# Two attention blocks on one core: the first 256 tokens transposed on TensorE, weight and x loads rescheduled

## The chip, the core and the metric

The kernel runs on one core of a Trainium2 chip. The metric is the time of one execution on the device, in microseconds (us). The core's engines run side by side and wait for each other through semaphores: TensorE (PE) multiplies and transposes, its weight loads shown apart as PEld; VectorE (DVE) and ScalarE (ACT) work on SBUF and PSUM; GpSimd (POOL) only makes an identity matrix here; the sync engine's queue (SPq) issues every DMA, plain copies and DMA transposes alike, in one order.

## The reference

Two independent attention blocks, A and B, of equal shapes; their outputs stand side by side in the last dimension.

```python
# per block: x [8, 144, 640], k_cache and v_cache [8, 32, 512, 128], wq [640, 4096], wo [4096, 640], bf16
q = (x @ wq).reshape(B, Sq, H, Dh).transpose(0, 2, 1, 3)
scores = einsum("bhqd,bhkd->bhqk", q, k_cache) * (Dh ** -0.5)
p = softmax(scores, axis=-1)
o = einsum("bhqk,bhkd->bhqd", p, v_cache)
return o.transpose(0, 2, 1, 3).reshape(B, Sq, H * Dh) @ wo
```

Each K and each V head is used once, for 144 queries, so the caches (2 x 2 x 33.5 MB) are streamed from HBM.

## The kernel before

The work is cut into 64 groups: block, then batch, then four groups of eight heads. So groups 0 to 31 are block A and 32 to 63 block B, and four groups make one batch. A group does the following (`attention_group`, L380):

- four projections of two heads each, ten matmuls into `ps_q` (L396), scaled into `qt_sb` by ScalarE (L407). They read a quarter of wq (`wq_sb`, one quarter for each g) and the transposed x (`xT_sb`, five chunks of 128 features by 1152 tokens);
- scores of 128 queries for each head (L483), and of the last 16 queries of all eight heads together (L425, eight small matmuls, once in a group);
- the row maximum on VectorE (L355), the exponential on ScalarE (L359), reciprocal and scaling on VectorE (L371, L376);
- transposes of the probabilities on TensorE into `ps_pt` (L504, L450), copied out by VectorE (L520, L465);
- the product with V into `ps_o` (L531), copied out by ScalarE (L544, L545).

The output projection of a batch (`outproj_ops`: L578 for the first 512 columns, L593 for the last 128, copies at L605 and L611, stores at L619 and L625) is cut into small items, which a queue hands out as filler between the attention steps, one at every second call of `fill`. The last 16 queries of all eight batches are projected together as one more "remainder" at the end of each block.

Loads go through four helpers: `load_wq` (L288, issue at L294), `load_wo` (L298, L304), `load_xT` (L308, L315: five DMA transposes of 576 tokens, half of a block's) and `load_kv` (L321: for each of the two halves of a group one DMA transpose of four K heads, L335, and one plain load of four V heads, L340). K has a ring of four slots, that is two groups; V has six.

No order is written out by hand. Every operation is handed to a small planner (`_Sched`) with what it reads and writes, an estimated duration, and a priority that is mostly its number in the program. The planner fixes, before the launch, the order of each engine's instructions and of the DMA queue, looking over the next 24 of each. On the chip each engine works through its list and waits on semaphores; an issue whose buffer is not free holds back everything behind it on the DMA queue.

Where the weight and x loads stand in the program decides their place in the queue:

- start: `load_xT(0, 0)`, then wq quarter 0 of A, then K and V of group 0; wq quarter g ahead of group g (L655 to L658);
- the second half of A's xT ahead of group 12 (L660); wo quarter hg of A ahead of group 4 + hg (L662);
- wq quarter g of B right behind group 28 + g (L705);
- the first half of B's xT behind group 15 (L707), the second half behind group 31 (L709), that is just ahead of group 32;
- the four wo quarters of B as queue items behind the whole remainder of A (L710 to L712).

Of the kernel before, what the change touches and what calls it, by code (L numbers as in the profile page):

```python
# [22 lines left out]
NPT_BANKS = 2  # L23
SCHED_WINDOW = 24
MODEL_ONLY = False
PRIO = {"OPa": 150, "OPb": 150, "Qp": -40, "Qe": -40}
OPA_HEADS = 4
FILL_STRIDE = 2
OPB_HEADS = 8
_DBG = {}  # L30

# [24 lines left out]
class _Sched:  # L56
# [36 lines left out]
    def schedule(self, engines, window=24):  # L93
# [22 lines left out]
        while remaining:  # L116
            best = None
            for e in engines:
                lst = per_eng[e]
                n = len(lst)  # L120
                cnt = 0
                i = pos[e]
                cand = None
                tf = t_eng[e]
                while i < n and cnt < window:
                    oi = lst[i]
                    if not done[oi]:
                        cnt += 1
                        rt = ready_time(ops[oi])
                        if rt < INF:  # L130
                            if rt + LEAD <= tf:
                                cand = (tf, oi, 0.0)
                                break
                            st = rt if rt > tf else tf
                            if cand is None or st < cand[0] - 1e-9:
                                cand = (st, oi, PENALTY.get(e, 0.0))
                    i += 1
                if cand is not None and (best is None or cand[0] < best[0] - 1e-9):
                    best = (cand[0], cand[1], e, cand[2])
# [37 lines left out]
def bass_concat_heads__gqa_block_cached__mha_block_cached__near_ridge_kernel(  # L177
# [34 lines left out]
    XH = 2 if NB % 2 == 0 else 1  # L212
    BPH = NB // XH

    NK = 4
    NV = 6
    NP = 8
    NT = 12
    NQG = 2
    NOB = 2  # L220
    NOS = 2

    S = _Sched()

    with ExitStack() as st:
# [36 lines left out]
        for e in ("pe", "act", "dve", "pool"):  # L262
            sem(("eng", e))

        def setup_ops():
            def f_ones(g):
                return g.memset(ones_sb[:], 1.0)
# [17 lines left out]
                                        for g in range(NG) for pi in range(4)],  # L285
                  dur=_dve_ns(2 * H * 128, 4), name="zero_otr")

        def load_wq(blk, hg):  # L288
            wq = blks[blk][3]
            src = wq.rearrange("(c p) n -> p c n", p=128)[:, :, hg * 1024:(hg + 1) * 1024]  # L290
            dst = wq_sb[:, :, hg * 1024:(hg + 1) * 1024]

            def f(e):
                return e.dma_start(dst, src)  # L294
            S.add("sp", f, writes=[("wq", hg)], dur=200, dma=(("wq", hg), 128 * NCH * 1024 * 2, "pl"),
                  name="wq%d.%d" % (blk, hg))

        def load_wo(blk, hg):  # L298
            wo = blks[blk][4]
# [5 lines left out]
            S.add("sp", f, writes=[("wo", hg)], dur=200, dma=(("wo", hg), 128 * 8 * D * 2, "pl"),  # L305
                  name="wo%d.%d" % (blk, hg))

        def load_xT(blk, half):  # L308
            x = blks[blk][0]
            xf = x.rearrange("b q d -> (b q) d")  # L310
            t0 = half * BPH * SQ
            t1 = (half + 1) * BPH * SQ
            for c in range(NCH):
                def f(e, c=c):
                    return e.dma_start_transpose(xT_sb[:, c, t0:t1], xf[t0:t1, c * 128:(c + 1) * 128])  # L315
                S.add("sp", f, writes=[("xT", half, c)], dur=200,
                      dma=(("xT", half, c), (t1 - t0) * 256, "tr"), name="xT%d.%d.%d" % (blk, half, c))

        kv_ctr = [0]

        def load_kv(blk, b, g):  # L321
            kc = blks[blk][1]
            vc = blks[blk][2]
            slots = []
            for s2 in range(2):
                h0 = 8 * g + 4 * s2
                kslot = kv_ctr[0] % NK
                vslot = kv_ctr[0] % NV
                kv_ctr[0] += 1
                slots.append((kslot, vslot))  # L330
                ksrc = kc[b, h0:h0 + 4].rearrange("h k d -> (h k) d")
                vsrc = vc[b, h0:h0 + 4].rearrange("h (p c) d -> p h (c d)", p=128)

                def fk(e, kslot=kslot, ksrc=ksrc):
                    return e.dma_start_transpose(kt_sb[:, kslot, :], ksrc)  # L335
                S.add("sp", fk, writes=[("KT", kslot)], dur=200, dma=(("KT", kslot), 4 * SK * 256, "tr"),
                      name="K%d.%d.%d.%d" % (blk, b, g, s2))

                def fv(e, vslot=vslot, vsrc=vsrc):
                    return e.dma_start(v_sb[:, vslot, :, :], vsrc)  # L340
                S.add("sp", fv, writes=[("V", vslot)], dur=200, dma=(("V", vslot), 4 * SK * 256, "pl"),
                      name="V%d.%d.%d.%d" % (blk, b, g, s2))
            return slots

        tile_ctr = [0]
        sbank_ctr = [0]
        ptbank_ctr = [0]

        def softmax_me(sbank, tag):
            ts = tile_ctr[0] % NT  # L350
            pslot = (tile_ctr[0] // 1) % NP
            tile_ctr[0] += 1

            def f_m(v):
                return v.tensor_reduce(nm_sb[:, ts:ts + 1], ps_s[:, sbank, :], AXL.X, ALU.max, negate=True)  # L355
            S.add("dve", f_m, reads=[("PSS", sbank)], writes=[("nm", ts)], dur=_dve_ns(512), name="M" + tag)

            def f_e(a):
                return a.activation(p_sb[:, pslot, :], ps_s[:, sbank, :], ACTF.Exp,  # L359
                                    bias=nm_sb[:, ts:ts + 1], scale=1.0, accum_out=rs_sb[:, ts:ts + 1])  # L360
            S.add("act", f_e, reads=[("PSS", sbank), ("nm", ts)], writes=[("P", pslot), ("rs", ts)],
                  dur=_act_ns(512, 1, True), name="E" + tag)
            return ts, pslot

        def softmax_rn(tiles, tag):
# [7 lines left out]
                  writes=[("rr", t0 + i) for i in range(n)], dur=68 + 2 * n, name="R" + tag)  # L373
            for i, (ts, pslot) in enumerate(tiles):
                def f_n(v, ts=ts, pslot=pslot):
                    return v.tensor_scalar(p_sb[:, pslot, :], p_sb[:, pslot, :], rr_sb[:, ts:ts + 1], None, ALU.mult)  # L376
                S.add("dve", f_n, reads=[("rr", ts), ("P", pslot)], writes=[("P", pslot)],
                      dur=_dve_ns(512, 4, 1), name="N%s.%d" % (tag, i))

        def attention_group(blk, b, g, gi, fill, heads_done):  # L380
            gs = gi % NQG
            bs = b % NOB
            slots = load_kv(blk, b, g)
            half = b // BPH
            tg = "%d.%d.%d" % (blk, b, g)

            for pi in range(4):
# [3 lines left out]
                def f_qp(t, pi=pi):  # L391
                    ins = None
                    for uu in range(2):
# [6 lines left out]
                                start=(c == 0), stop=(c == NCH - 1),  # L400
                            )
                    return ins
                S.add("pe", f_qp, reads=[("wq", g)] + [("xT", half, c) for c in range(NCH)],
                      writes=[("PSQ",)], dur=2 * NCH * _mm_ns(SQ), name="Qp%s.%d" % (tg, pi))

                def f_qe(a, pi=pi, off=off):
# [147 lines left out]
        def outproj_ops(blk, b, acc=None, acc_res=("PSOUT",)):  # L554
# [33 lines left out]
            def mk_b(k):  # L588
                def go():
                    def f(t):  # L590
                        ins = None
                        for h in range(OPB_HEADS * k, OPB_HEADS * (k + 1)):
                            ins = t.matmul(acc[:, 0:D2], lhs(h), wo_sb[:, h, 512:D],  # L593
                                           start=(h == 0), stop=(h == H - 1))
                        return ins
# [56 lines left out]
            load_wo(blk, hg)  # L652
            wo_loaded.add((blk, hg))

        before(0, lambda: load_xT(0, 0))  # L655
        before(0, lambda: load_wq(0, 0))
        for g in range(1, NG):
            before(g, lambda g=g: load_wq(0, g))  # L658
        if XH == 2:
            before(BPH * NG - NG, lambda: load_xT(0, 1))  # L660
        for hg in range(NHG):
            before(NG + hg if NB > 1 else NG - 1, lambda hg=hg: do_load_wo(0, hg))  # L662

        queues = [[], []]

# [21 lines left out]
        for blk in range(2):  # L687
            for b in range(NB):
# [6 lines left out]
                for g in range(NG):  # L695
# [3 lines left out]
                        queues[1].extend(outproj_ops(blk, NB, acc=ps_q, acc_res=("PSQ",)))  # L699
                    fill_state[0] = 0  # L700
                    fill_state[1] = FILL_STRIDE
                    attention_group(blk, b, g, gi, fill, heads_done)
                    gi += 1
                    if blk == 0 and b == NB - 1:
                        load_wq(1, g)  # L705
                if blk == 0 and XH == 2 and b == BPH - 1:
                    load_xT(1, 0)  # L707
                if blk == 0 and b == NB - 1:
                    load_xT(1, XH - 1)  # L709
                    queues[0].extend(outproj_ops(blk, NB))  # L710
                    for hg in range(NHG):
                        queues[0].append((1, -1, 0, None, lambda hg=hg: do_load_wo(1, hg), NB - 1))  # L712
        heads_done[(1, -1)] = 0
        while queues[0] or queues[1]:
            if not pop_filler():
# [27 lines left out]
        for o in ops:  # L743
            if o.dma is not None and o.dma[0][0] in ("out", "outr"):
                out_final[o.done_key] = max(out_final.get(o.done_key, 0), o.done_val)

        def emit(ename, eng):
            waited = {}
            for oi in order[ename]:
                o = ops[oi]  # L750
                needs = {}
                for p, kind in o.preds.items():
                    po = ops[p]
                    if po.dma is None and po.eng == ename:
                        if ename == "pe":
                            continue
                        if kind != "raw":
                            continue
                    if needs.get(po.done_key, 0) < po.done_val:
                        needs[po.done_key] = po.done_val  # L760
                for key, val in needs.items():
                    if waited.get(key, 0) >= val:
                        continue
                    eng.wait_ge(sems[key], val)
                    waited[key] = val
                ins = o.fn(eng)
                ins.then_inc(sems[o.done_key], 16 if o.dma is not None else 1)
            if ename == "sp":
                for key, val in out_final.items():
                    eng.wait_ge(sems[key], val)  # L770
# [48 lines left out]
```

## Time and profile before

| | |
|---|---|
| time, median of 3 runs | 792.96 us (791.12 to 794.85) |
| span of the profiled run | 791.8 us |
| ScalarE busy | 613.9 us (78%) |
| VectorE busy | 719.9 us (91%) |
| DMA | 162.59 MB, mean 205 GB/s |
| K loads | 128 DMA transposes of 512 KB |
| V loads | 128 plain copies of 512 KB |
| wq and wo loads | 16 of 1280 KB, 6.5 to 9.7 us from issue to landing |
| x loads | 20 DMA transposes, 2.8 to 9.9 us from issue to landing |

How to read it: "busy" is the time in which an engine has an instruction running. A wait is charged to what released it last, as far as the profile can tell. The page also divides the span into 40 equal slices, each digit the busy share in tenths; a stretch view gives the same for any part of the run, with TensorE's granted clock (1.00 is full), the share of time that the 16 DMA engines were busy, and GB/s. In the DMA queue's list an issue's duration contains the time for which it was held back, whether by a semaphore or by a full queue. A matmul row gives the number of instructions merged into it and, in brackets, the idle time ahead of it and its releaser.

### The profile page before, as it was taken

The numbers are of one execution on the slowest core, as the hardware profiler recorded it, in microseconds if no ns is written. First come the engines' busy times: TensorE is split into PE (matmuls) and PEld (weight loads), VectorE is DVE, ScalarE is ACT, GpSimd is POOL, SyncE is SP. The second block draws the span as 40 slices with busy tenths as digits, with TensorE's granted clock in tenths as the row PEclk, the third lists the DMA queues.
The fourth block names the chain that finished last, engine by engine and source line by source line (L and its number), as shares of the span: only waits on it lengthen the run. The fifth ranks groups of instructions, "written<-read, shape, count | busy, mean of one in ns | idle before, by whom it ended". The sixth has DMA issues, their size and how long they took to land.

```text
span 791.8 us, 23122 instructions
## 1 busy us (share of the span) xinstructions
PE 748.4 (95%) x9088; PEld 566.8 (72%) x9088; DVE 719.9 (91%) x1858; ACT 613.9 (78%) x1957; POOL 0.7 (0%) x6
## 2 busy tenths in 40 slices
PE   2788799999999999999979999999999999999997
PEld 1566567677778777878757767777777778787864
DVE  2798889989999999999969879999999999999992
ACT  1678678778888888888858768888888888888873
POOL 0000000000000000000000000000000000000000
PEclk9999999999999999999989999999999999999999
DMA  7999999999998978899999899988888888889730
GB/s 183 265 237 284 237 259 231 205 223 211 206 215 193 191 194 187 195 231 265 244 223 218 217 276 236 232 190 203 172 193 193 207 177 206 184 192 200 185 36 18
DMA packets 362476, 162.59 MB, mean 205 GB/s; under 512 B 281216, under 2 KB 357248, under 8 KB 362368
## 3 DMA queue, kind: packets, MB, share of 16 engines
q1 hardware_dynamic: 362368, 161.12, 91.8%
q8 instruction: 72, 1.18, 0.7%
q14 instruction: 36, 0.29, 0.1%
HBM read 88.08 MB, written 2.95 MB: 115 GB/s over the span
## 4 chain that ended last, share of the span: by engine, by line
PE 85%; DMA 9%; DVE 4%; ACT 1%; SPq 1%; issue 0%; ACTq 0%
PE ps_q L396 19%; PE ps_o L531 15%; PE ps_out L578 14%; PE ps_pt L504 13%; PE ps_s L483 13%; DMA kt_sb<-in_A_k_cache_dram 5%; PE ps_s L425 4%; PE ps_out L593 4%; DMA kt_sb<-in_B_k_cache_dram 2%; DVE nm_sb L355 2%; PE ps_pt L450 2%; PE ps_q L578 1%; DMA wo_sb<-in_B_wo_dram 1%; DMA wq_sb<-in_A_wq_dram 1%; SPq L315 1%; DVE ptg_sb L520 1%
## 5 line engine op out<-in xcount | busy, mean ns | idle before, releaser
L359 ACT ACTIVATE p_sb<-ps_s,nm_sb 128x512 bf16<-128x512 f32 x576 | 397.6, 697 | 60.4 <-DVE nm_sb L355 44.9
L355 DVE TENSOR_REDUCE nm_sb<-ps_s 128x1 f32<-128x512 f32 x576 | 384.0, 678 | 29.9 <-PE ps_s L483 20.1
L396 PE MATMUL ps_q<-xT_sb,wq_sb 128*128 128x144 bf16 x2560 | 206.0, 229 | 15.8 <-DMA wq_sb<-in_A_wq_dram 14.1
L396 PEld LDWEIGHTS ps_q<-xT_sb,wq_sb 128*128 128x128 bf16 x2560 | 174.0, 99 | 50.5 <-DMA wq_sb<-in_A_wq_dram 14.1
L520 DVE COPY ptg_sb<-ps_pt 128x1024 bf16<-128x1024 bf16 x256 | 174.9, 686 | 22.5 <-PE ps_pt L504 20.0
L483 PE MATMUL ps_s<-kt_sb,qt_sb 128*128 128x512 bf16 x512 | 184.7, 382 | 10.2 <-ACT p_sb L359 4.5
L376 DVE TENSOR_SCALAR p_sb<-p_sb,rr_sb 128x512 bf16<-128x512 bf16 x576 | 180.4, 346 | 1.4
L531 PE MATMUL ps_o<-ptg_sb,v_sb 128*128 128x144 bf16 x2048 | 171.3, 227 | 0.8 <-DVE ptg_sb L465 0.4
L531 PEld LDWEIGHTS ps_o<-ptg_sb,v_sb 128*128 128x128 bf16 x2048 | 138.9, 98 | 35.8 <-DVE ptg_sb L520 10.9
L504 PE MATMUL ps_pt<-id_sb,p_sb 128*128 128x128 bf16 x2048 | 156.6, 220 | 2.9 <-DVE p_sb L376 2.8
L407 ACT ACTIVATE qt_sb<-ps_q 128x288 bf16<-128x288 f32 x256 | 107.0, 418 | 55.6 <-PE ps_q L396 52.4
L504 PEld LDWEIGHTS ps_pt<-id_sb,p_sb 128*128 128x128 bf16 x2048 | 132.6, 114 | 24.2 <-DVE p_sb L376 10.8
L578 PE MATMUL ps_out<-wo_sb,otm_sb 128*128 128x512 bf16 x512 | 131.4, 379 | 0.9 <-DMA wo_sb<-in_B_wo_dram 0.9
L544 ACT CAST otm_sb<-ps_o 128x256 bf16<-128x256 f32 x256 | 95.1, 371 | 46.5 <-PE ps_o L531 42.7
L359 ACT ACTIVATION_READ_ACCUMULATOR p_sb<-ps_s,nm_sb 128x1 f32 x576 | 120.4, 209 | 0.0
L578 PEld LDWEIGHTS ps_out<-wo_sb,otm_sb 128*128 128x128 bf16 x512 | 48.5, 98 | 44.8 <-issue 1.3
L483 PEld LDWEIGHTS ps_s<-kt_sb,qt_sb 128*128 128x128 bf16 x512 | 47.7, 98 | 27.1 <-ACT p_sb L359 11.3
L371 DVE RECIPROCAL rr_sb<-rs_sb 128x2 f32<-128x2 f32 (+1 forms) x320 | 50.2, 157 | 3.4 <-ACT p_sb L359 2.5
L545 ACT CAST otr_sb<-ps_o 128x32 bf16<-128x32 f32 x256 | 50.3, 197 | 0.0
L425 PE MATMUL ps_s<-kt_sb,qt_sb 128*32 128x512 bf16 x512 | 39.8, 388 | 6.4 <-DMA kt_sb<-in_B_k_cache_dram 6.2
L593 PE MATMUL ps_out<-wo_sb,otm_sb 128*128 128x128 bf16 x512 | 38.8, 219 | 0.0
L593 PEld LDWEIGHTS ps_out<-wo_sb,otm_sb 128*128 128x128 bf16 x512 | 32.3, 98 | 7.5 <-issue 2.5
(25 smaller groups left out, 135.7 us busy)
## 6 DMA issues: line engine op xcount, KB each, us to landing
v_sb<-in_A_v_cache_dram SPq DMA_DIRECT2D x64, 512.0 KB, 4.6
v_sb<-in_B_v_cache_dram SPq DMA_DIRECT2D x64, 512.0 KB, 4.4
wq_sb<-in_A_wq_dram SPq DMA_DIRECT2D x4, 1280.0 KB, 7.9
wo_sb<-in_A_wo_dram SPq DMA_DIRECT2D x4, 1280.0 KB, 8.0
wq_sb<-in_B_wq_dram SPq DMA_DIRECT2D x4, 1280.0 KB, 7.2
wo_sb<-in_B_wo_dram SPq DMA_DIRECT2D x4, 1280.0 KB, 8.1
out_dram<-ost_sb SPq DMA_DIRECT2D x16, 160.0 KB, 3.9
kt_sb<-in_A_k_cache_dram SPq DMA_TRANSPOSE x64, 5.9
```

What stands on the lines that cost most here:

```text
L355: return v.tensor_reduce(nm_sb[:, ts:ts + 1], ps_s[:, sbank, :], AXL.X, ALU.max, negate=True)
L359: return a.activation(p_sb[:, pslot, :], ps_s[:, sbank, :], ACTF.Exp, bias=nm_sb[:, ts:ts + 1], scale=1.0, accum_out=rs_sb[:, ts:ts + 1])
L376: return v.tensor_scalar(p_sb[:, pslot, :], p_sb[:, pslot, :], rr_sb[:, ts:ts + 1], None, ALU.mult)
L396: ins = t.matmul(ps_q[:, uu * SQ:(uu + 1) * SQ], wq_sb[:, c, h * 128:(h + 1) * 128], xT_sb[:, c, b * SQ:(b + 1) * SQ], start=(c == 0), sto ...
L407: return a.mul(qt_sb[:, gs, 2 * pi:2 * pi + 2, off:off + SQ], ps_q[:, 0:2 * SQ].rearrange("p (u q) -> p u q", u=2), SCALE,)
L483: return t.matmul(ps_s[:, sbank, :], qt_sb[:, gs, u, qoff:qoff + 128], kt_sb[:, slot, (u % 4) * SK:(u % 4 + 1) * SK], start=True, stop=True,)
L504: ins = t.transpose(ps_pt[:, kpt, (uu * 4 + c) * 128:(uu * 4 + c + 1) * 128], pv[:, c, :], id_sb[:],)
L520: return v.tensor_copy(dst, src)
L531: ins = t.matmul(ps_o[:, uu * SQ:(uu + 1) * SQ], v_sb[:, slot, u % 4, c * 128:(c + 1) * 128], ptg_sb[:, gs, u, c, :], start=(c == 0), stop ...
L544: a.copy(otm_sb[:, bs, h0:h0 + 2, :], src[:, :, 0:128])
L578: ins = t.matmul(acc[:, 0:512], lhs(h), wo_sb[:, h, 0:512], start=(h == 0), stop=(h == H - 1))
L593: ins = t.matmul(acc[:, 0:D2], lhs(h), wo_sb[:, h, 512:D], start=(h == 0), stop=(h == H - 1))
```

## The change

It has four parts, and a number of constants (ring sizes, sizes for experiments, relays) which keep their present values.

1. The start. Of A's first 576 tokens, the first 256 are no longer transposed by DMA. They are loaded plainly into `ost_sb`, the output's staging buffer, which is unused at that time; TensorE transposes them in ten blocks of 128 x 128 into the two banks of `ps_pt`, and VectorE copies them to `xT_sb`. The other 320 tokens are still transposed by DMA, now ahead of group 1. wq's first quarter follows the plain load directly. The aim is an earlier first projection.
2. wq of B: quarter g goes ahead of group 30 + g, one group later than before.
3. xT of B, second half: ahead of group 44 and no longer ahead of group 32. The aim is to keep it out of the way of block B's first K.
4. wo of B: each quarter is queued as soon as the remainder's second pass has used the old quarter, between the items of that pass.

```diff
+        NXA = 256 if (XT_PE and BPH * SQ >= 256 and SQ <= 256) else 0
+        def load_x_pe():
...
+            stage = ost_sb
...
+                return e.dma_start(stage[:, 0:nt, :], xf[0:NXA, :].rearrange("(t p) d -> p t d", p=128))
...
+                    for j, (c, t) in enumerate(chunk):
+                        ins = t_.transpose(ps_pt[:, kpt, j * 128:(j + 1) * 128],
+                                           stage[:, t, c * 128:(c + 1) * 128], id_sb[:])
...
+                    return v.tensor_copy(
+                        xT_sb[:, c0:c0 + nc_, 0:NXA],
+                        ps_pt[:, kpt, 0:nc_ * NXA].rearrange("p (c k) -> p c k", c=nc_),
+                    )
...
-        before(0, lambda: load_xT(0, 0))
-        before(0, lambda: load_wq(0, 0))
+        if NXA:
+            before(0, load_x_pe)
+            for pi in range(4):
+                before(0, lambda pi=pi: load_wq(0, 0, pi))
+            before(XT_REST_AT, lambda: load_xT(0, 0, skip=NXA))
...
                     if blk == 0 and b == NB - 1:
-                        load_wq(1, g)
+                        for pi in range(4):
+                            tgt = max(gi, NB * NG + g - WQB_LEAD)
+                            (after if WQ_INTERLEAVE else before)(tgt, lambda g=g, pi=pi: load_wq(1, g, pi))
...
                 if blk == 0 and b == NB - 1:
-                    load_xT(1, XH - 1)
-                    queues[0].extend(outproj_ops(blk, NB))
+                    if XH == 2:
+                        before(NB * NG + (BPH - 1) * NG, lambda: load_xT(1, 1))
...
+                    queues[0].extend(head)
+                    for k, it in enumerate(passb):
+                        queues[0].append(it)
+                        for hg in range(NHG):
+                            if (hg * 8) // OPB_HEADS == k and ((hg + 1) * 8 - 1) // OPB_HEADS == k:
+                                queues[0].append((1, -1, 0, None, lambda hg=hg: do_load_wo(1, hg), NB - 1))
+                    queues[0].extend(tail_)
```

`load_wq` is called for four pieces, but with `WQ_PIECES = 1` only the first call issues, and it loads the whole quarter as before. `XT_REST_AT` is 1 and `WQB_LEAD` is 2.

## The prediction

> **What bounds the kernel now.** I read the page first for the shares and slices, then the waits of TensorE, then stretches of 2 to 10 us, then the DMA queue and the pieces of work in order of time.
>
> From the page, parts 1 and 2 (busy time; then the 40 slices of 19.8 us):
>
> ```profile
> span 791.8 us, 23122 instructions
> PE 748.4 (95%) x9088; PEld 566.8 (72%) x9088; DVE 719.9 (91%) x1858; ACT 613.9 (78%) x1957; POOL 0.7 (0%) x6
> ...
> PE   2788799999999999999979999999999999999997
> ```
>
> TensorE is the bound: busy 748.4 of 791.8 us, full in most slices. Whatever gains must come out of the 43.4 us that it idles, or out of work done slowly. The low slices are the first five, one near 400 us, and the last. The waits of the whole run (engine, line, releaser: total us, times, longest) name them:
>
> ```profile
> PE ps_q L396 <- DMA wq_sb<-in_A_wq_dram: 14.1, 1, 14.1
> ...
> PE ps_s L425 <- DMA kt_sb<-in_B_k_cache_dram: 6.2, 2, 5.2
> ...
> PE ps_out L578 <- DMA wo_sb<-in_B_wo_dram: 0.9, 1, 0.9
> ```
>
> One wait of 14.1 us before the first matmul; one of 5.2 us (and one of 1.0) for a K transpose of block B; 0.9 us for wo of B. The stretches of 10 us (PE, PEld, DVE, ACT, POOL busy, then PE clock, DMA share, GB/s) give the idle time by stage: 30.5 us before 120 us, 5.2 between 390 and 410, 1.9 between 450 and 480, 6.0 at the end, none elsewhere.
>
> ```profile
> 0.00:10.00 10.00, 0.00 (x0) 0.00 (x0) 4.60 (x2) 1.28 (x1) 0.70 (x6) 1.00 0.51 97
> 10.00:20.00 10.00, 5.27 (x35) 3.79 (x36) 1.01 (x2) 1.56 (x4) 0.00 (x0) 1.00 1.04 266
> ...
> 400.00:410.00 10.00, 7.12 (x70) 5.45 (x71) 3.59 (x9) 2.96 (x11) 0.00 (x0) 0.66 1.01 230
> ```
>
> In the first 10 us the DMA engines are half idle (share 0.51, 97 GB/s); from 10 to 120 us they run full, at 200 to 294 GB/s. At 400 us the clock has dropped to 0.66. The DMA queue's own instructions show why:
>
> ```profile
> 0.80 6.46 SPq L315 DMA_TRANSPOSE xT_sb<-in_A_x_dram  x5
> 7.31 0.58 SPq L294 DMA_DIRECT2D wq_sb<-in_A_wq_dram  x1
> 7.94 5.87 SPq L335 DMA_TRANSPOSE kt_sb<-in_A_k_cache_dram  x1
> ...
> 384.09 10.55 SPq L315 DMA_TRANSPOSE xT_sb<-in_B_x_dram  x5
> 394.74 5.84 SPq L335 DMA_TRANSPOSE kt_sb<-in_B_k_cache_dram  x2
> ```
>
> The first wq waits 6.5 us for five x transposes to be issued, and the first K of block B waits 10.55 us behind five more, whose tokens are not needed before batch 4 of B. TensorE then stands still until:
>
> ```profile
> 402.88 1.05 PE L425 MATMUL ps_s<-kt_sb,qt_sb 128*32 128x512 bf16 x8 [5.19 <-DMA kt_sb<-in_B_k_cache_dram]
> ```
>
> From 7 to 112 us the queue never pauses: each group of eight heads brings two K, two V and one wq or wo, and takes about 13.4 us (K of group 1 at 19.58, of group 7 at 100.04). Later a group takes 11.2 us on TensorE, the mean interval of L425 from group 16 (205.76) to 31 (385.56). So **the start is paced by the DMA stream, the rest by TensorE**. A trap: the queue's waits put 6.6 us before the K at 19.58 on TensorE, but that K fills its ring slot for the first time (slot 2 of 4) and has nothing to wait for. It is the full stream holding back the issue; the smallest K issue in the run is 1.63 us.
>
> **What the Trainium skill says.** "DMA: Bandwidth & Descriptors", Queues, rings and completion order: each DMA engine consumes descriptors in ring order, so what is queued first delays all behind it. The trace agrees (K behind 10.55 us of x). The same page, Latency and other measured facts, gives 261 GB/s for a DMA transpose; here, with x alone, 103 to 118 GB/s flow between 2 and 8 us, so I use the trace. "TensorE: Matmul & The Clock Gate", Part 1: an idle array falls to half clock and needs about 3.4 us of work to come back. The trace agrees: ten L396 matmuls take 1.20 us in the chain at 405 us and 0.62 at 407.5.
>
> **The change part by part.**
>
> *Start.* The five transposes leave the head of the queue; one plain load of 256 tokens (328 KB) takes their place, one issue, 0.58 us as for V. wq's issue moves from 7.31 to about 1.4 us, 5.9 us earlier; with its own 6.7 us to landing (7.31 to 14.03) it lands at 8.1. Beside it: ten TensorE transposes at the cold rate, 8 in 0.64 us after 22.98, so 0.8 us; two PSUM copies, 0.69 us for 1024 columns (L520) and 0.24 for 256 (L465). VectorE runs them behind its two memsets, which end at 6.54, so xT is ready at about 7.5, before wq. This costs nothing: wq's flight hides it. The first matmul starts 6.0 us earlier.
>
> That is not yet a gain, since the stream behind paces groups 1 to 8. The remaining 320 tokens come as five transposes ahead of group 1's wq. They are needed only at group 4, but stand before wq, K and V. Two bounds: **by bytes**, 410 KB at the 258 GB/s of this stage is 1.6 us, leaving 5.9 - 1.6 = 4.3 us; **by issue**, 576 rows cost 1.27 us and 2048 rows at least 1.63, so 320 rows about 1.2, five 6.0 us, leaving 0. In between: when these five begin (13.1 us) about 4 us of K and V are still queued, which run meanwhile; then the engines thin out, and group 1's wq goes out at 19.1 against 19.03 before, but on a nearly empty queue: 6.7 us to landing, the run's minimum, against a median of 7.5 and a maximum of 9.7. That is 0.8 to 3 us earlier; I take 1.5.
>
> *wq of B.* Moved one group later, still two groups (22 us) ahead of use, landing in under 10 us: 0. It also takes one wq out from in front of B's first K.
>
> *xT of B, second half.* Moved from before group 32 to before group 44, for use in group 48. Removed: the 5.19 us stall, and the slow clock after it. In the chain, L425, L531, two L483, L396, L504 take 1.05 + 1.07 + 0.43 + 1.20 + 0.68 = 4.43 us; at full clock 0.57 + 0.50 + 0.22 + 0.62 + 0.45 = 2.36. So 2.1 more: 7.3 in all. Check: groups 32 and 33 take 17.32 + 13.27 = 30.6 us against 2 x 11.2 = 22.5, an excess of 8.1. K of group 32 can be issued about 383 us and land near 392, and L425 would want it at 397.7. I take 7.0. At its new place five issues of 1.3 to 2.1 us (6.4 to 10.6) stand ahead of group 44's K. That K's slot comes free about 18 us before use, and the same five issues at 202.56 (6.43 us) left TensorE full from 200 to 220: 0.
>
> *wo of B.* Interleaved with the remainder's second pass rather than behind all of it: each wo is issued some 2 to 8 us sooner and the output rows no longer sit between them. There are 0.87 us of wo wait and 0.99 of K wait to win; but four wo are 5.2 MB in a row in front of a K. I take 1.3.
>
> The other edits (constants, ring sizes, relays with no engine) add no instruction. Sum: 1.5 + 7.0 + 1.3 = 9.8; 792.96 - 9.8 = **783**.
>
> **The rivals.**
>
> *The bytes count alone.* The backlog keeps the engines full through the five issues: 4.3 + 7.3 + 1.8 = 13.4, so 779.6. For it: this stage moves 200 to 294 GB/s while issues wait. Against: between 152 and 156 us, with xT issued in a row, it fell to 137 GB/s. If the whole 6.0 of the start stays, with the 8.1 of the check and 1.9 of wo, 777.0.
>
> *The start gives all back and the stall only shrinks.* K of group 32 still comes 3 us late behind wq, with the clock drop: 0 + 3.5 + 0.5 = 4.0, so 789. Against: without xT, K has some 6 us in hand.
>
> *Stalls move.* The split x load adds 0.2 us to the stream (0.6 + 6.0 against 6.46), x of B delays group 44's K as it did group 32's (7.3 lost again), and wo in a row holds up K of group 37 by 5 us more: 793 + 0.2 + 5 = 798, slower. For it: 11.75 us for two K behind two wo at 460.69. Against: TensorE has filler there and idled only 0.99 us.
>
> **How the numbers follow.** Forecast 0.62, bytes alone 0.20, shrunken stall 0.11, moved stalls 0.07. The time is the first, 783. The range runs from 776.5 to 789.5: from the most that the parts can give, 777.0, to the shrunken stall, with half a microsecond beyond each for the measurement. It leaves out the last case and some tail. Faster by over 0.5% means below 789.0: the first two, and half of the third, 0.87; same 0.07; slower 0.06.
>
> **What would show it.** First matmul near 8 us; x transposes on the queue at about 13 to 19 us; group 1's wq issued near 19 and landing near 26; L425 of group 7 a little before 113.95; no wait of L425 on block B's K near 390 us and no clock below 1.0 there; interval of groups 32 and 33 near 11 us each; TensorE full at group 44. It is wrong if the start's lead is still 4 us or more at group 7 (bytes), if L425 stalls on K at group 32, 37 or 44, or if TensorE's busy time changes by more than a few us.

## The result, and the profile after

The changed kernel takes 788.31 us in the median (785.39 to 791.57, 12 runs) beside 793.05 us for the kernel before (791.12 to 798.02, 15 runs): a ratio of 0.9934, interval 0.9913 to 0.9955. So it is faster, by 4.7 us. That lies in the range on record, but it is half of the 9.8 us that the sum promised, and it lies next to the 789 of the third case ("the start gives all back and the stall only shrinks"). The profiled execution took 791.0 us, near the slow end of its twelve, so its span alone understates the gain.

Page of the changed kernel, busy times and slices:

```profile
span 789.3 us, 23174 instructions
...
PE 752.0 (95%) x9098; PEld 570.3 (72%) x9098; DVE 721.4 (91%) x1860; ACT 614.7 (78%) x1957; POOL 0.7 (0%) x6
...
PE   4888799999999999999989999999999999999997
```

The first slice rose from 2 to 4 and the dip near 400 us, in the same slice, shrank from 7 to 8. TensorE is 3.6 us busier than before, of which the ten new transposes are 1.25; what the rest is was not followed up.

Waits of TensorE in the changed kernel (engine, line, releaser: total us, times, longest). L509 is the former L425, L479 the former L396:

```profile
PE ps_s L509 <- DMA kt_sb<-in_B_k_cache_dram: 5.0, 3, 3.2
...
PE ps_pt L375 <- DMA ost_sb<-in_A_x_dram: 3.9, 1, 3.9
...
PE ps_q L479 <- DMA wq_sb<-in_A_wq_dram: 3.4, 2, 2.7
```

The 14.1 us ahead of the first projection became 3.9 + 2.7 us. But block B's K still stops TensorE: 5.0 us in all against 6.2, its longest wait 3.2 against 5.2. And a second wait for wq of A has appeared (0.77 us, at 25.32).

The order of the DMA queue in the changed kernel (start, duration, line, what), first at the start, then at block B's first K:

```profile
0.81 0.46 SPq L362 DMA_DIRECT2D ost_sb<-in_A_x_dram  x1
1.32 0.45 SPq L317 DMA_DIRECT2D wq_sb<-in_A_wq_dram  x1
...
12.62 6.32 SPq L350 DMA_TRANSPOSE xT_sb<-in_A_x_dram  x5
18.99 0.58 SPq L317 DMA_DIRECT2D wq_sb<-in_A_wq_dram  x1
...
383.29 5.48 SPq L412 DMA_TRANSPOSE kt_sb<-in_B_k_cache_dram  x1
...
389.45 0.50 SPq L317 DMA_DIRECT2D wq_sb<-in_B_wq_dram  x1
390.04 9.92 SPq L412 DMA_TRANSPOSE kt_sb<-in_B_k_cache_dram  x2
```

The five x transposes of block B are gone from the front of K. In their place wq's last quarter now goes out **between the two K of group 32**.

TensorE and VectorE in order of time:

```profile
6.46 0.82 DVE L384 COPY xT_sb<-ps_pt 128x1024 bf16<-128x1024 bf16 x2
7.82 1.38 PE L479 MATMUL ps_q<-xT_sb,wq_sb 128*128 128x144 bf16 x10 [2.66 <-DMA wq_sb<-in_A_wq_dram]
...
400.21 0.62 PE L509 MATMUL ps_s<-kt_sb,qt_sb 128*32 128x512 bf16 x8 [3.17 <-DMA kt_sb<-in_B_k_cache_dram]
```

The chain of waits, followed through the same place, says which K that was: the one issued second, 10 us in flight.

```profile
390.04 10.03 DMA kt_sb<-in_B_k_cache_dram
400.07 0.14 issue
400.21 0.62 PE ps_s L509 x8
```

Stretches of 10 us of the changed kernel (length, PE, PEld, DVE, ACT, POOL busy, TensorE clock, DMA share, GB/s), and then one of the kernel before, whose two earlier stretches stand in the prediction:

```profile
0.00:10.00 10.00, 2.92 (x23) 2.37 (x24) 5.33 (x4) 1.69 (x2) 0.70 (x6) 1.00 0.83 229
10.00:20.00 10.00, 7.08 (x52) 4.15 (x49) 5.30 (x11) 4.50 (x12) 0.00 (x0) 1.00 0.76 185
20.00:30.00 10.00, 7.86 (x72) 6.64 (x72) 6.07 (x19) 4.79 (x16) 0.00 (x0) 0.66 0.97 249
...
390.00:400.00 10.00, 7.04 (x92) 5.69 (x89) 7.60 (x19) 7.45 (x24) 0.00 (x0) 1.00 0.98 257
400.00:410.00 10.00, 9.79 (x98) 7.43 (x99) 7.26 (x20) 4.95 (x15) 0.00 (x0) 0.83 1.09 229
```

```profile
20.00:30.00 10.00, 6.37 (x51) 3.98 (x48) 7.74 (x21) 6.23 (x19) 0.00 (x0) 0.91 1.04 270
```

Over 10 us, 229 GB/s are 2.29 MB, so the last column can be read as megabytes. Before moved 0.97 + 2.66 = 3.63 MB in 20 us, after 2.29 + 1.85 = 4.14. A lead of 1.32 MB at 10 us is 0.5 MB at 20 us; by 30 us (2.70 against 2.49 more) it is 0.3 MB, 1.2 us at the 258 GB/s of this stage. The third row shows TensorE at 0.66 of its clock in the changed kernel, where before had 0.91.

The same in terms of L509/L425, which runs once in a group:

| start of that matmul in group | 0 | 1 | 4 | 7 | 31 | 33 | 35 | 38 | 63 |
|---|---|---|---|---|---|---|---|---|---|
| before, us | 23.6 | 36.9 | 74.7 | 114.0 | 385.6 | 416.1 | 438.5 | 481.3 | 763.2 |
| after, us | 17.4 | 33.1 | 72.3 | 113.1 | 385.6 | 412.5 | 436.7 | 478.0 | 761.3 |

The lead of 6.2 us in group 0 is down to 0.9 by group 7. From group 9 to group 30 every kernel of this study has the same intervals to 0.01 us in nearly every group, so what a front (the part of the run up to there) is worth is settled by group 9. The second gain comes at groups 32 and 33, and part of it is given back at 34 and 35.

### The profile page after: what moved, and what is told of

Same layout as the page of the kernel before. It is cut to its first block, busy times and chain, and to the rows that moved or that the text cites. A ratio compares the mean times of both kernels' runs of the same rounds, so it can differ in the third digit from the quotient of the medians.

```text
span 789.3 us, 23174 instructions
## 1 busy us (share of the span) xinstructions
PE 752.0 (95%) x9098; PEld 570.3 (72%) x9098; DVE 721.4 (91%) x1860; ACT 614.7 (78%) x1957; POOL 0.7 (0%) x6
## 4 chain that ended last, share of the span: by engine, by line
PE 82%; DMA 11%; DVE 3%; SPq 3%; ACT 1%; issue 0%; ACTq 0%
PE ps_q L479 17%; PE ps_o L615 15%; PE ps_out L662 13%; PE ps_pt L588 13%; PE ps_s L567 12%; DMA kt_sb<-in_A_k_cache_dram 7%; PE ps_s L509 4%; PE ps_out L680 4%; DMA kt_sb<-in_B_k_cache_dram 3%; PE ps_pt L534 2%; DVE nm_sb L435 1%; SPq L412 1%; PE ps_q L662 1%; DMA wq_sb<-in_A_wq_dram 1%; SPq L350 1%; DVE ptg_sb L604 1%
## 5 line engine op out<-in xcount | busy, mean ns | idle before, releaser
L441 ACT ACTIVATE p_sb<-ps_s,nm_sb 128x512 bf16<-128x512 f32 x576 | 397.7, 696 | 63.9 <-DVE nm_sb L435 41.5
L479 PE MATMUL ps_q<-xT_sb,wq_sb 128*128 128x144 bf16 x2560 | 206.5, 229 | 5.4 <-DMA wq_sb<-in_A_wq_dram 3.4
L479 PEld LDWEIGHTS ps_q<-xT_sb,wq_sb 128*128 128x128 bf16 x2560 | 174.3, 99 | 39.8 <-ACT qt_sb L491 10.4
L567 PE MATMUL ps_s<-kt_sb,qt_sb 128*128 128x512 bf16 x512 | 186.3, 384 | 9.8 <-DMA kt_sb<-in_A_k_cache_dram 4.5
L491 ACT ACTIVATE qt_sb<-ps_q 128x288 bf16<-128x288 f32 x256 | 106.8, 417 | 54.5 <-PE ps_q L479 52.2
L662 PE MATMUL ps_out<-wo_sb,otm_sb 128*128 128x512 bf16 x512 | 131.3, 379 | 0.0
L628 ACT CAST otm_sb<-ps_o 128x256 bf16<-128x256 f32 x256 | 94.9, 371 | 42.2 <-PE ps_o L615 38.5
L662 PEld LDWEIGHTS ps_out<-wo_sb,otm_sb 128*128 128x128 bf16 x512 | 48.6, 98 | 44.5 <-issue 1.7
L567 PEld LDWEIGHTS ps_s<-kt_sb,qt_sb 128*128 128x128 bf16 x512 | 48.2, 98 | 25.9 <-ACT p_sb L441 8.5
L629 ACT CAST otr_sb<-ps_o 128x32 bf16<-128x32 f32 x256 | 50.2, 196 | 0.0
L509 PE MATMUL ps_s<-kt_sb,qt_sb 128*32 128x512 bf16 x512 | 39.4, 384 | 7.0 <-DMA kt_sb<-in_B_k_cache_dram 5.0
```

The source lines that it names most:

```text
L441: return a.activation(p_sb[:, pslot, 0:EXP_E_COLS], ps_s[:, sbank, 0:EXP_E_COLS], ACTF.Exp, bias=nm_sb[:, ts:ts + 1], scale=1.0, accum_out ...
L479: ins = t.matmul(ps_q[:, uu * SQ:(uu + 1) * SQ], wq_sb[:, c, h * 128:(h + 1) * 128], xT_sb[:, c, b * SQ:(b + 1) * SQ], start=(c == 0), sto ...
L491: return a.mul(qt_sb[:, gs, 2 * pi:2 * pi + 2, off:off + SQ], ps_q[:, 0:2 * SQ].rearrange("p (u q) -> p u q", u=2), SCALE,)
L567: return t.matmul(ps_s[:, sbank, :], qt_sb[:, gs, u, qoff:qoff + 128], kt_sb[:, slot, (u % 4) * SK:(u % 4 + 1) * SK], start=True, stop=True,)
L628: a.copy(otm_sb[:, bs, h0:h0 + 2, :], src[:, :, 0:128])
L662: ins = t.matmul(acc[:, 0:512], lhs(h), wo_sb[:, h, 0:512], start=(h == 0), stop=(h == H - 1))
```

## The experiments

My theory after the result: the start's lead is eaten by the five short x transposes, and block B's stall is not gone because its stream, with four wq in it, is full even without x. The rival explanations: the start's lead is lost to the mere bytes of x, or in the first groups whatever is loaded; block B's remaining stall is due to wq's new place; what moving x saved comes back where wo is loaded.

Line numbers shift by a few lines, or some thirty, from kernel to kernel; the operands tell which instruction it is. All kernels of this section ran beside the kernel before, in three sets, each on another chip: start_only, b_only, plain_rest and wq_spread (the kernel before: 789.76 us), after_again, no_rest, wq_spread2 and x_move_only (790.62), and wq_as_before, wo_as_before, both2 and both3 (790.2). So compare ratios across sets, not times. One table for all; the two columns on the right are stretches of TensorE's time between the starts of L509 in groups 31, 35 and 38, from the one profiled execution of each:

| kernel | us | ratio to before | interval | 31 to 35 | 35 to 38 |
|---|---|---|---|---|---|
| before | | 1 | | 52.9 | 42.8 |
| after | 788.31 | 0.9934 | 0.9913 to 0.9955 | 51.1 | 41.3 |
| after_again | 786.52 | 0.9952 | 0.9934 to 0.9970 | 52.2 | 41.2 |
| start_only | 791.26 | 1.0021 | 1.0006 to 1.0036 | 52.0 | 43.1 |
| b_only | 784.25 | 0.9937 | 0.9912 to 0.9962 | 47.6 | 41.5 |
| no_rest | 778.59 | 0.9857 | 0.9833 to 0.9881 | 47.9 | 41.1 |
| plain_rest | 784.25 | 0.9929 | 0.9908 to 0.9951 | 50.0 | 42.2 |
| x_move_only | 786.13 | 0.9946 | 0.9925 to 0.9966 | 46.0 | 46.9 |
| wq_as_before | 786.51 | 0.9966 | 0.9954 to 0.9979 | 48.3 | 44.0 |
| wq_spread | 791.08 | 1.0009 | 0.9994 to 1.0023 | 50.2 | 44.3 |
| wq_spread2 | 785.07 | 0.9942 | 0.9919 to 0.9965 | 45.2 | 45.4 |
| wo_as_before | 787.55 | 0.9976 | 0.9960 to 0.9993 | 48.7 | 44.4 |
| both2 | 781.06 | 0.9904 | 0.9873 to 0.9935 | 44.8 | 43.0 |
| both3 | 784.09 | 0.9930 | 0.9903 to 0.9956 | 46.1 | 42.5 |

One number for the noise of a single profile: kernels whose first 120 us are the same code (before, b_only, x_move_only) reached group 7 at 114.0, 111.2 and 110.3 us. So one profile of each doesn't compare two fronts. Taken together, the profiles give the start of L509 in group 7, in the mean of the kernels that share a front:

| front | profiles | group 7, us | range |
|---|---|---|---|
| of the kernel before | 3 | 111.8 | 110.3 to 114.0 |
| changed (after, after_again, start_only, wq_as_before, wq_spread, wq_spread2, wo_as_before) | 7 | 111.7 | 109.8 to 114.1 |
| rest loaded plainly (plain_rest, both2, both3) | 3 | 109.8 | 108.9 to 110.2 |
| rest left out (no_rest) | 1 | 105.1 | |

By these means the changed start is worth nothing at group 7; the lead of 0.9 us in the first pair of profiles lies within their scatter.

### The two halves apart: start_only and b_only

start_only keeps part 1 of the change and puts block B's loads back to where they were; b_only is the reverse.

```diff
 # start_only                                    # b_only
-  before(tgt, ... load_wq(1, g, pi))            -XT_PE = True
+  load_wq(1, g, pi)                             +XT_PE = False
-  before(NB*NG + (BPH-1)*NG, load_xT(1, 1))     -XT_FIRST = False
+  load_xT(1, XH - 1)                            +XT_FIRST = True
-  ... wo items between those of passb ...
+  ... wo items behind the whole remainder ...
```

> The changed start alone, with block B's loads placed as in the kernel before. My theory: groups 1 to 8 are paced by the DMA stream and the five remaining x transposes cost it about as much as their removal from the head gave, so the lead of 6 us at group 0 shrinks to 1 us at group 7 and the time falls by 0.5 to 2 us, to 791 to 792.5 us. Rival (the start is worth its full 6 us and the changed kernel lost it later, in block B): the time falls by 5 to 6 us, to 787.

> Block B's rescheduling alone, with the start as in the kernel before. My theory: it carries most of the measured gain, 3 to 4 us (789 to 790 us): the wait of L425 on K at group 32 falls from 5.2 to about 3 us, not to zero, and the clock loss shrinks with it. Rival (the gain came from the start): 0 to 1 us, 792 to 793.

Measured: the start alone doesn't make the kernel faster, as I had expected, but **slower**, by 0.0021 x 790 = 1.6 us (0.5 to 2.8), although its first projection begins at 8.5 us. The profiles, with 111.7 beside 111.8 us at group 7, do not show where such a loss would be: no gain is shown, a small loss only by the timed runs. Block B's part alone gives 0.9937, and the two together, 1.0021 x 0.9937 = 0.9958, agree with the changed kernel (0.9934 and 0.9952) within the intervals. So all of the gain comes from block B.

### What eats the start: no_rest, plain_rest

no_rest leaves the five transposes of the other 320 tokens out; batches 1 to 3 of block A project batch 0's tokens in their place, and nothing else differs. plain_rest brings the same bytes as two plain loads, and transposes them on TensorE.

```diff
 # no_rest
-  before(XT_REST_AT, lambda: load_xT(0, 0, skip=NXA))
-  xT_sb[:, c, b * SQ:(b + 1) * SQ]
+  xT_sb[:, c, xb * SQ:(xb + 1) * SQ]        # xb = 0 for b < 4 of block A
 # plain_rest
-  before(XT_REST_AT, lambda: load_xT(0, 0, skip=NXA))
+  before(XT_REST_AT, load_x_rest)   # 2 plain loads to xs_sb, 15 transposes, 5 copies
```

> The changed kernel without the five transposes of the remaining 320 tokens: batches 1 to 3 of block A project the tokens of batch 0 instead, and nothing else is left out. If these five transposes eat the lead: the lead at group 1 grows from 3.8 to about 6 us, at group 7 it is 4 to 6 us, and the time is 4 to 6 us below the changed kernel's. If the lead is lost on TensorE (cold clock, the chain of group 0) or in the later stream whatever stands there: under 1.5 us below.

> The changed kernel, with the remaining 320 tokens loaded plainly too and transposed on TensorE: the same bytes in the same place of the stream, two issues in place of five transposes. If it is the transposes (their issue time and their low rate) that eat the lead: at group 7 the lead over the kernel before is about 4 us in place of 0.9, and the time is 3 to 4 us below the changed kernel's, near 785. If it is the bytes: nothing changes, 788. If the lead is lost on TensorE (cold clock, chains of group 1): 788 or a little more, since 15 more transposes run there.

Measured: no_rest is 7.5 us faster than after_again of the same set (0.9952 - 0.9857, times 790.6; some 5 to 10 us by the two intervals), and 6.6 us ahead of the mean of the changed fronts at group 7. Its bytes would explain 1.6 us of that (410 KB at 258 GB/s). The stretches from 10 to 30 us show more; no_rest, then plain_rest, where the changed kernel had share 0.76 and 185 GB/s, then 0.97 and 249:

```profile
10.00:20.00 10.00, 7.67 (x54) 3.93 (x52) 4.53 (x9) 4.05 (x11) 0.00 (x0) 0.89 1.00 291
20.00:30.00 10.00, 8.84 (x97) 6.78 (x97) 7.64 (x21) 6.73 (x21) 0.00 (x0) 0.77 1.05 248
```

```profile
10.00:20.00 10.00, 6.67 (x51) 4.07 (x49) 5.47 (x12) 4.80 (x13) 0.00 (x0) 1.00 1.04 292
20.00:30.00 10.00, 8.97 (x107) 7.67 (x107) 6.77 (x19) 5.83 (x18) 0.00 (x0) 0.83 1.16 190
```

As five transposes the 410 KB thin the stream out: 106 GB/s less over 10 us are 1.06 MB, 4.1 us of this stage's stream. As plain loads they leave it full for these 10 us, but in the next 10 us all three kernels with plain loads move only 190, 181 and 205 GB/s, with the DMA engines busy; why is not shown. By 30 us no_rest had moved 7.55 MB, these three 7.1 to 7.2 and the seven with transposes 6.4 to 6.7; 0.41 MB of that is x in all but no_rest. So in everything but x the plain loads put the stream some 0.8 MB behind no_rest and the transposes some 1.4 MB, 3.2 and 5.3 us at 258 GB/s. That is near what the fronts differ by at group 7, 4.7 and 6.6 us.

The queue's own rows for those five in the changed kernel, and for the five of 576 tokens in the kernel before (duration in ns: least, median, most):

```profile
L350 SPq DMA_TRANSPOSE xT_sb<-in_A_x_dram x5: 1170/1247/1247, 12.6 to 17.7; - x5
```

```profile
L315 SPq DMA_TRANSPOSE xT_sb<-in_A_x_dram x5: 1233/1259/1267, 0.8 to 6.0; - x5
```

320 tokens cost the queue as much as 576. Shortening the transposes therefore saved bytes and no queue time, and the hole in the stream delayed group 1's wq (issued at 18.99, at 13.58 in no_rest) and every K behind it.

plain_rest is at 0.9929 where b_only of the same set is at 0.9937: with it the start costs nothing, and gains next to nothing either. I had expected 3 to 4 us over the changed kernel; it is 0.4 to 1.8 (against after and after_again). Part of its lead goes in group 6, as its row shows (a wait for K of block A):

```profile
92.35 0.61 PE L599 MATMUL ps_s<-kt_sb,qt_sb 128*128 128x512 bf16 x2 [3.40 <-DMA kt_sb<-in_A_k_cache_dram]
```

both2, with the same front, lost it there too (group 6 took 17.0 us), both3 did not (11.8 us), and yet all three reached group 9 at 129.3 to 129.6 us.

So both theories have a share, and mine has the smaller one: the form of the load is worth some 2 us of the 6.6 to 7.5 (1.9 at group 7), and most of it goes with loading these tokens at this place in either form. 1.6 us of that are bytes; the other 3 or so are not explained, and the 15 further TensorE transposes and 5 copies of plain_rest were not tested by themselves.

### What moving x is worth: x_move_only

The kernel before, with this one edit of the change:

```diff
-  load_xT(1, XH - 1)
+  before(NB*NG + (BPH-1)*NG, lambda: load_xT(1, 1))
```

> The kernel before with one edit: the second half of B's x goes ahead of group 44 rather than 32. In the changed kernel's queue the wq of B are issued at nearly the same times as before, since the planner looks 24 issues ahead and takes what is ready; so wq's new place should be worth nothing, wo's at most 1 us, and this one edit carries the gain of block B: 4 to 5 us, ratio 0.994 to 0.995. Rival (wq's or wo's place matters too): under 3 us, 0.9965 or more.

Measured: 0.9946, 4.3 us (2.7 to 5.9). In its profile it saves up to group 35 what was forecast for this step, 46.0 us against 52.9. There is no wait at group 32, and TensorE is full from 375 to 425 us. Then 4.1 us come back by group 38. Its waits of TensorE from 375 to 500 us, and its queue just ahead:

```profile
PE ps_s L509 <- DMA kt_sb<-in_B_k_cache_dram: 3.7, 1, 3.7
PE ps_out L662 <- DMA wo_sb<-in_B_wo_dram: 0.5, 1, 0.5
```

```profile
448.25 1.86 SPq L327 DMA_DIRECT2D wo_sb<-in_B_wo_dram  x2
450.17 12.94 SPq L412 DMA_TRANSPOSE kt_sb<-in_B_k_cache_dram  x2
```

The kernel before, at the same place:

```profile
460.69 11.75 SPq L335 DMA_TRANSPOSE kt_sb<-in_B_k_cache_dram  x2
```

Two K stand behind the last wo in both, and begin 7.6 us after L509 of group 36 in both. In x_move_only they take 1.2 us longer, and TensorE wants K of group 37 1.2 us sooner after group 36, so it waits 3.69 us where it waited 0.99. After that the clock is at 0.83 from 460 to 470 us, and group 38 takes 11.0 us instead of 8.4. From group 31 to the end of the profile 3.4 us are left (402.9 against 406.2), which fits the timed 4.3. In the six profiles of this study with at most 1.6 us of K wait at group 32, the wait at 37 is 1.2 to 3.7 us; in the eight others it is 0.9 to 2.1. So part of a stall that goes at 32 tends to come back at 37; how much varies from profile to profile.

### Where wq goes: wq_as_before, wq_spread, wq_spread2

wq_as_before is the changed kernel with wq of B back in its old place. The two others put the quarters 1, 2 and 3 of wq behind a TensorE instruction (L425 of the named group in the numbering of before), so that the planner can't draw them together.

```diff
 # wq_as_before
-  (after if WQ_INTERLEAVE else before)(tgt, lambda: load_wq(1, g, pi))
+  load_wq(1, g, pi)
 # wq_spread: quarters 0..3 ahead of groups 29, 31, 33, 35
+  before((29, 31, 33, 35)[g], lambda: load_wq(1, g, 0, after_sr=(None, 29, 31, 33)[g]))
 # wq_spread2
+  before((29, 31, 33, 34)[g], lambda: load_wq(1, g, 0, after_sr=(None, 29, 31, 32)[g]))
```

> The changed kernel with the wq of B placed as in the kernel before, one group earlier. In the changed kernel wq 3 goes out between the two K of group 32, and L425 waits 3.1 us there; where only x was moved, wq 3 goes out ahead of both and L425 does not wait. If wq's new place is what kept the stall: no wait at group 32, groups 32 and 33 take about 23 us (27 to 28 now). Part of it should come back at groups 37 and 38, where the four wo stand ahead of K (K wait of 2 to 4 us), so the time is 0 to 2.5 us below the changed kernel's: ratio 0.992 to 0.995. Rival (K is late there whatever the order): the wait of 3 us stays.

> The changed kernel, with wq quarters 1 to 3 of B made to wait for L425 of groups 29, 31 and 33, so that no two of them are issued within one group and none stands between the two K of group 32. If the remaining wait at group 32 comes from wq 3 (and the run of four wq) ahead of K: L425 of group 32 waits under 0.5 us, groups 32 and 33 take 23 to 24 us in place of 26.9, and the time is about 3 us below the changed kernel's, 785. If K of group 32 is late for another reason: the wait stays at 3 us and the time at 788.

> As wq_spread, but wq 3 waits for L425 of group 32 and no longer of 33, since there the projection of group 35 waited 3.2 us for it. If the four wq in a row were the rest of the stall at group 32: no wait of L425 at 32 and none of L479 on wq of B, groups 32 to 35 take 45 to 47 us together (51 in the changed kernel's profile, 49.5 in that of b_only), and the time is 2 to 4 us below the changed kernel's. If the stall only moves with the bytes: K or wq waits of 2 us or more appear again somewhere in groups 32 to 36, and the time is that of the changed kernel.

Measured: wq's old place gains nothing in the time (0.9966, beside 0.9934 and 0.9952 for the changed kernel: 1.1 to 2.5 us slower if anything, with intervals that overlap); my expectation of a gain failed. The rows of wq_as_before show the wait at 32 smaller, and the one at 37 larger:

```profile
396.13 0.62 PE L509 MATMUL ps_s<-kt_sb,qt_sb 128*32 128x512 bf16 x8 [1.55 <-DMA kt_sb<-in_B_k_cache_dram]
407.72 0.61 PE L509 MATMUL ps_s<-kt_sb,qt_sb 128*32 128x512 bf16 x8 [0.60 <-DMA kt_sb<-in_B_k_cache_dram]
466.22 0.61 PE L509 MATMUL ps_s<-kt_sb,qt_sb 128*32 128x512 bf16 x8 [2.69 <-DMA kt_sb<-in_B_k_cache_dram]
```

That is 4.8 us of K waits, against 4.4 in the changed kernel in the same stretch and 3.7 in x_move_only. All profiles together show what wq's place does. With wq between the two K of group 32 (the changed kernel twice, b_only, no_rest, plain_rest, wo_as_before) TensorE waits 1.7 to 3.2 us there; with x moved and wq ahead of both K (x_move_only, wq_as_before, both3) 0, 1.6 and 0. But groups 31 to 38 take 91.5 us in the mean of the six and 91.2 in that of the three: here the order of the loads decides where TensorE waits, and hardly how long the stretch takes.

wq_spread takes the K wait at 32 away, but held wq's last quarter so long that a projection stopped for it, and was not faster than the kernel before, where I had expected 3 us less than the changed kernel:

```profile
420.73 0.80 PE L482 MATMUL ps_q<-xT_sb,wq_sb 128*128 128x144 bf16 x10 [3.23 <-DMA wq_sb<-in_B_wq_dram]
```

wq_spread2 releases that quarter one group sooner. It has the shortest groups 31 to 35 but for both2 (45.2 us), and the K wait then comes at group 37, 2.0 us. Its 0.9942 can't be told from after_again's 0.9952, where I had expected 2 to 4 us less.

How full the stream is there is in the profile of the kernel before, in a stretch that I had not read. Its row from 345 to 375 and from 375 to 395 us:

```profile
345.00:375.00 30.00, 30.00 (x382) 23.37 (x379) 29.58 (x78) 25.94 (x82) 0.00 (x0) 1.00 1.02 256
375.00:395.00 20.00, 20.00 (x235) 14.81 (x232) 19.37 (x52) 16.06 (x54) 0.00 (x0) 1.00 1.16 254
```

TensorE is full, and so are the DMA engines, 50 us ahead of the stall. By an estimate from the start's figure, four groups with a wq each are four groups of 13.4 us of stream under 11.2 us of TensorE, so the queue loses some 9 us there. That leaves little room for anything more ahead of K; but x_move_only, with the same four wq ahead, has no K wait at group 32, so these alone don't make that K late.

### wo's place: wo_as_before

```diff
-  ... wo items between those of passb ...
+  ... wo items behind the whole remainder ...
```

> The changed kernel with the wo of B behind the whole remainder, as in the kernel before. If the interleaved wo is worth what I forecast (1.3 us) or more: a wait of 0.5 to 1 us for wo returns, K waits 1 to 4 us at group 37 or 38, and the time is 1 to 3 us above the changed kernel's, ratio 0.9965 to 0.999. Rival: no difference, 0.995.

Measured: 0.9976 against 0.9952 of after_again: by that the interleaving is worth about 1.9 us, with intervals that overlap a little. The profiles don't show it: from group 31 to the end of the span wo_as_before takes 403.0 us, the changed kernel 403.7 and 403.9. So what wo's place is worth is not settled. Its waits for K at 32 and 37 are 2.2 and 1.8 us, but L662 and L567 add waits for ScalarE (1.2 and 0.4 us) that the changed kernel does not have there.

### The repeat and the two combinations

after_again is the changed kernel unaltered. both2 joins plain_rest and wq_spread2, both3 joins plain_rest and wq_as_before.

> The changed kernel itself, for comparison on the same chip. 0.993 of the kernel before was measured; with block B's part alone at 0.9937 and the start alone at 1.0021, the sum of the parts is 0.9958. If the parts add up: 0.995 to 0.997; if they help each other: 0.993.

> plain_rest and wq_spread2 together: the remaining tokens loaded plainly, wq 1 to 3 of B spread by waits. If the two gains add up (1.8 and 0.8 us beyond the changed kernel): ratio about 0.992. If the stall at 37 and 38 takes the second back: 0.993, as plain_rest alone. In the front, a lead of 7 us at group 5 over the kernel before, with 1.6 to 2 us less than without the rest at all (9.3), by bytes; whether group 6 takes 16.7 us again (a K wait of 3.4 us and the clock drop after it) or 12 shows whether that loss belongs to the kernel or to the execution.

> plain_rest together with wq_as_before: the remaining tokens loaded plainly, wq of B at its old place. If the wait at group 32 is due to wq's new place: none there, and a ratio of 0.991 to 0.993. Group 6 as for both2: 12 us if the loss of 4 us in plain_rest's profile was that execution's, 16 to 17 if it is the kernel's.

Measured: both2 is at 0.9904, 781.06 us beside 790.2. Against the mean of the two measurements of the changed kernel (0.9943) that is 0.0039 less, with an interval of 0.0034 on the difference: faster than both kernels, if narrowly for the second. both3 is 2.4 us faster than wq_as_before of the same set, so a plain load of the rest does gain 2 to 3 us over the transposes. In both2 only one K wait is left in this stretch of block B:

```profile
PE ps_s L544 <- DMA kt_sb<-in_B_k_cache_dram: 1.9, 1, 1.9
```

## Why the prediction was half right

**The start's first steps held.** The flight of wq, from its issue to its landing, hid the transposes: the first projection began at 7.82 us (forecast 8.1), xT was ready at 7.28 (7.5), the five transposes went out from 12.62 to 18.94 (13 to 19), and group 1's wq at 18.99 (19.1). The ten transposes took 1.25 us (0.8).

**The step that failed is the last of the start: "I take 1.5"**, that is, a cost of 5.9 - 1.5 = 4.4 us for the five short transposes. Leaving them out gained 7.5 us in the timed runs and 6.6 at group 7, so they took the whole 5.9 us of lead. The bound "by issue" (6.0 us, 6.32 measured on the queue) was the right size, and the credit given against it was wrong: the DMA engines ran at 0.76 of their time from 10 to 20 us, TensorE stopped for group 1's wq and worked on at 0.66 of its clock. The start is worth nothing by the profiles and -1.6 us by the timed runs, not +1.5. The argument that the nearly empty queue would bring wq sooner held (6.3 us from issue to the end of the wait, 6.7 forecast) and didn't matter; the K behind it were as late as before (19.61 us, 19.58 before). The Trainium skill gives 261 GB/s for a DMA transpose ("DMA: Bandwidth & Descriptors", Latency and other measured facts); an estimate from it is 1.6 us for 410 KB. Their issue alone took 6.32 us, which is 65 GB/s. The measurement decides.

**xT of B: right at its place, 7.0 forecast, 6.9 found in the profile of x_move_only.** But 4.1 us of it return at groups 35 to 38 of that profile, and 4.3 are left in the time. I treated the stall as alone. The third rival of the prediction named the queue of K behind wo, and I dismissed it because TensorE "idled only 0.99 us" there. In x_move_only K came later and TensorE sooner, by some 1.2 us each, which makes most of the 3.69.

**wq of B: 0 held in the time, to within 1 to 3 us; the words beside it failed.** "It also takes one wq out from in front of B's first K": it put that wq between the two K of group 32. And "K of group 32 can be issued about 383 us and land near 392" was true of the first K (383.29). L425 takes all eight heads, so it needs the second too, which was issued at 390.04 and landed at 400.07. That made the remaining wait of 3.17 us, the third case's "3 us late behind wq". So one of the signs by which the prediction called itself wrong came true: L425 stalled on K at group 32 (3.17 us) and at 37 (1.23). And the clock, which was not to fall below 1.0 there, fell to 0.83. In "K has some 6 us in hand" I counted one K of two.

**Group 44: near 0.** TensorE was full from 540 to 560 us. The planner drew these loads forward, to 494.64 and 503.01 us, and there one K wait of 0.56 us (group 41) shows in the changed kernel and none in its repeat.

**wo of B: 1.3 forecast, about 1.9 by the timed runs, not seen in the profiles.**

The sum as it was found: -1.6 + 4.3 + 0 + 1.9 = 4.6 us, against 4.7 measured. That close an agreement is luck, since each term is known to 1 or 2 us only; b_only's 5.0 for all of block B gives 3.4. Direction and range held; of the cases the third came nearest, which I had given 0.11.

Three readings of the prediction were off without harm to its sum. "The smallest K issue in the run is 1.63 us" is true of block A; in block B one took 1.24 us (at 599.79), the same as 320 or 576 rows. The L425 at 205.76 us is that of group 15, and 16 intervals give the 11.2 us. The idle time before 120 us is 30.2 us, not 30.5.

What stays open: b_only and after_again differ in the front alone, yet their groups 31 to 38 take 89.1 and 93.4 us; no_rest, with a third front, takes 89.0. These profiles can't say whether the front reaches that far, or whether this is the variation from one execution to another; if it does, part of the 7.5 us of no_rest arises there. Nor was a version tried in which all of wo of B goes out between 425 and 450 us, where the changed kernel moves 202 GB/s at a share of 0.93 (in x_move_only two of the four did, at 438.69).

## What to carry to other kernels

A load moved out of the way of a stall can be worth less than the stall: here 6.9 us at its place became 4.3 in the time. Ask which wait an earlier TensorE will meet next, and read the share and GB/s of the stretches before and behind the stall. A wait for two tiles ends with the later one, so follow that. Shortening a DMA transpose from 576 to 320 rows saved no queue time; a plain load with TensorE transposes in its place gained some 2 us here, and leaving the load out altogether, which no_rest could do only by projecting other tokens, some 7.

## What was not expected of the hardware

- A DMA transpose of 320 tokens by 128 features occupies the queue for 1.25 us, one of 576 tokens for 1.26, and the shortest of K, with 2048 rows, for 1.24 (at 345.69 in the changed kernel). With five of the shorter ones the stream ran at 185 GB/s over 10 us, without them at 291; two plain loads of the same 410 KB (0.51 and 0.57 us to issue) left it at 292, but it then fell to 190 over the next 10 us.
- The front of one and the same code varied by 3.7 us between executions (group 7 at 110.3 to 114.0 us), while groups 9 to 30 repeated to 0.01 us in nearly every one. Here the stage paced by DMA needed several profiles or many timed runs; the one paced by TensorE could be read from one profile.
